# Two PSUM banks that exchange roles each group, eight output products in every slot, and first layers computed transposed

## Chip, cores, metric

The program runs on one core of a Trainium2 chip. The time is that of the device in microseconds. A ratio is the mean time of one kernel's fast runs over that of the kernel before in the same rounds, so it is not quite the ratio of the medians quoted. The kernel before had medians from 864.08 to 867.49 us in these rounds, so runs of different rounds are compared by their ratios.

## The reference, cut to what matters

```python
def mab(q, kv):                                   # softmax(q kv^T / sqrt(128)) kv
    ...
h = mab(inducing, x)                              # 4 batches, 32 rows of 128
x = mab(x, h)                                     # 4 x 12416 rows of 128
g, val = x @ w_gate, x @ w_val                    # 128 -> 1536 twice
ffn = (gelu(g) * val) @ w_out                     # 1536 -> 128
out = x + sigmoid(x @ w_res) * ffn
```

A row of the second attention's result is a mixture of 32 rows of `h`. So the kernel multiplies `h` by `w_gate`, `w_val` and `w_res` once a batch (the "first layers") and mixes the products with each token's 32 weights.

## The kernel before

Tokens go in groups of 512; a batch has 25 groups, its last a short one. A group has 12 chunks of 128 hidden columns, taken two at a time: six slots. A slot has a gate pair G (PE, then gelu `ge` on ACT), a value pair V (PE, then `u = ge*V` on DVE), and a share of the 48 output products `ffn += u.T @ wO`. Once a group PE also mixes rows for the sigmoid (`hr`, read by ACT as `th`) and for the residual (`ha`, read by ACT as `at`), and DVE forms `th = (th+1)*ffn`.

```python
ps_gv = ... bufs=3   # three tiles of two banks, shared by G, V and most else
ps_f  = ... bufs=1   # one bank: ffn
ps_m  = ... bufs=1   # one bank: mixes, accumulation of h, small work
...
for gi in range(ngrp):                            # f is the group's first slot
    ...
        at(f + 4, lg.gate)                        # mix for th, then th on ACT
        at(f + 6, lg.residual)                    # mix for at
        for i, n in enumerate((10, 10, 10, 9, 9)):
            at(f + 3 + i, lambda lg=lg, n=n: lg.mms(n))
        at(f + 7, lg.end)                         # th on DVE, add on POOL, store
...
bg(13 + i, 2, ...accumulate...)                   # bg(g, p): group g of the batch, slot p
bg(18, 2, finish_h); bg(19, 2, turn_h)
bg(20, 2, first_layer(hg, columns 0:1024)); bg(22, 2, first_layer(hv, 0:1024))
bg(23, 2, first_layer(hg and hv, 1024:1536)); bg(22, 5, res_layer)
...
            pe.matmul(bank[:, o:o + e - c], ht_t[b], w[:, c:e], start=True, stop=True)
                act.activation(dst[:, c0:c1], bank[:, o0:o], AC.Copy, bias=0.0, scale=0.5)
```

Products of a group stand in its slots 3, 4, 5 and in slots 0 and 1 of the next; slot 2 has none, and there the work for the next batch's `h` is put. Two bursts a batch compute all scores; after each, the number of gates that run ahead of values starts at one and grows by one every second group, up to four, so some groups have a seventh gate.

The softmax here doesn't subtract the row's maximum and nothing guards it: scores larger than these inputs give would overflow.

Of the kernel before, what the change touches and what calls it, by code (L numbers as in the profile page):

```python
# [18 lines left out]
def kernel(  # L19
# [49 lines left out]
    p_sm = ctx.enter_context(tc.tile_pool(name="soft", bufs=2))  # L69
    p_h = ctx.enter_context(tc.tile_pool(name="hpool", bufs=2))  # L70
    p_ge = ctx.enter_context(tc.tile_pool(name="gelu", bufs=6))
    p_u = ctx.enter_context(tc.tile_pool(name="up", bufs=8))
    p_fin = ctx.enter_context(tc.tile_pool(name="fin", bufs=2))
    ps_gv = ctx.enter_context(tc.tile_pool(name="psgv", bufs=3, space=bass.MemoryType.PSUM))
    ps_f = ctx.enter_context(tc.tile_pool(name="psf", bufs=1, space=bass.MemoryType.PSUM))
    ps_m = ctx.enter_context(tc.tile_pool(name="psm", bufs=1, space=bass.MemoryType.PSUM))

    ctx.enter_context(tc.manual_schedule())

    def misc_bank():  # L80
        return ps_m.tile([P, TOK], FP32, name="ms", tag="ms")

    def wide_bank():
        return ps_gv.tile([P, 2 * TOK], FP32, name="gv", tag="gv")
# [71 lines left out]
    def accumulate(b, j0, j1, first, last):  # L156
        if first:
            acc_t[b] = misc_bank()
        acc = acc_t[b]
        for j in range(j0, j1):  # L160
            k, jj = divmod(j, PRE)
            cq = j % Q
            o = acc[cq * M:(cq + 1) * M, :]
            e = e_of.pop(("a", b, j))
            pe.matmul(o[:, 0:P], e, hi_t[b, k][:, jj, :],
                      start=(first and j < j0 + Q), stop=False, skip_group_check=True)
            pe.matmul(o[:, P:2 * P + 1], e, lo_t[b, k][:, jj, :P + 1],
                      start=False, stop=(last and j + Q >= j1), skip_group_check=True)
        if last:
            if b not in nacc_t:  # L170
                nacc_t[b] = p_h.tile([P, 2 * P + 1], FP32, name="nacc", tag="nacc", bufs=1)
                ve.tensor_copy(nacc_t[b], acc[:, :2 * P + 1])
            else:
                na = nacc_t[b]
                ve.tensor_tensor(na, acc[:, :2 * P + 1], na, AL.add)
            del acc_t[b]

    def finish_h(b):
        hs = misc_bank()
        na = nacc_t.pop(b)  # L180
        sm = strips.rearrange("p q m -> p (q m)")
        pe.matmul(hs[:, P:P + 1], sm, na[:, 2 * P:2 * P + 1], start=True, stop=True)
        pe.matmul(hs[:, 0:P], sm, na[:, 0:P], start=True, stop=False)
        pe.matmul(hs[:, 0:P], sm, na[:, P:2 * P], start=False, stop=True)
        rz = p_h.tile([P, 1], FP32, name="rz1", tag="rz1")
        ve.reciprocal(rz, hs[:, P:P + 1])
        hf = p_h.tile([P, P], FP32, name="hf", tag="hf", bufs=1)
        ve.tensor_scalar(hf, hs[:, 0:P], rz, None, op0=AL.mult)
        hf_t[b] = hf
        ha = p_h.tile([P, P], FP16, name="ha", tag="ha")  # L190
        ha_t[b] = ha
        po.tensor_copy(ha, hf)
        po.tensor_tensor(ha[M:2 * M, :], hf[M:2 * M, :], ha[M:2 * M, :], AL.subtract)
        hg_t[b] = p_h.tile([P, F], BF16, name="hg", tag="hg")
        hv_t[b] = p_h.tile([P, F], BF16, name="hv", tag="hv")

    def turn_h(b):
        tp = misc_bank()
        pe.transpose(tp[:, :P], hf_t.pop(b), ident)
        ht = p_h.tile([P, P], FP16, name="ht", tag="ht")  # L200
        ve.tensor_copy(ht, tp[:, :P])
        ht_t[b] = ht

    def first_layer(b, parts, engs):
# [3 lines left out]
        for (dst, w, c0, c1), eng in zip(parts, engs):  # L208
# [7 lines left out]
            else:  # L216
                ve.tensor_scalar(dst[:, c0:c1], bank[:, o0:o], 0.5, None, op0=AL.mult)

    def res_layer(b):
        bank = misc_bank()  # L220
        pe.matmul(bank[:, :P], ht_t[b], wR, start=True, stop=True)
        hr = p_h.tile([P, P], FP16, name="hr", tag="hr")
        hr_t[b] = hr
        act.activation(hr, bank[:, :P], AC.Copy, bias=0.0, scale=1.0)
        ve.tensor_tensor(hr[M:2 * M, :], bank[M:2 * M, :P], hr[M:2 * M, :], AL.subtract)  # L225
# [82 lines left out]
    class Last:  # L308
# [9 lines left out]
        def mms(self, n):  # L318
            per = self.slots[0][1]
            for _ in range(min(n, len(self.todo))):  # L320
                fc, k = self.todo.pop(0)
                first = self.ffn is None
                if first:
                    self.ffn = ps_f.tile([P, TOK // P, P], FP32, name="ffn", tag="ffn")
                si, c = divmod(fc, per)
                o = c * self.tw + k * P

                pe.matmul(self.ffn[:, k, :], u_t[self.gi, si][:, o:o + P], wO[:, fc, :],  # L328
                          start=first, stop=not self.todo, skip_group_check=True)
                if k == self.nk - 1 and (c == per - 1 or fc == FCH - 1):  # L330
                    del u_t[self.gi, si]

        def mix(self, h):
            bank = misc_bank()
            r = slice(0, 2 * M)
            for k in range(self.nk):
                pe.matmul(bank[:, k * P:(k + 1) * P],  # L337
                          rt_t[self.b, self.k][r, self.j0 + k, :],
                          h[r, :], start=True, stop=True)
            return bank  # L340
# [108 lines left out]
    for j0 in range(PRE, nblk, 4 * PRE):  # L449
        j1 = min(j0 + 4 * PRE, nblk)  # L450
        norm_b(0, j0, j1, exp_b(0, j0, j1))
    warm = ps_f.tile([P, TOK // P, P], FP32, name="ffn", tag="ffn")
    for i in range(10):
        pe.matmul(warm.rearrange("p k c -> p (k c)"), wG[:, :P], wG[:, :TOK],
                  start=True, stop=True)



# [9 lines left out]
    bursts = {}  # L468
    LEAD = 4

    def at(i, f):
        windows.setdefault(i, []).append(f)

    for gi in range(ngrp):
        lg = Last(gi)
        f = first[gi]
        if len(groups[gi][4]) == 6:
            at(f + 4, lg.gate)
            at(f + 6, lg.residual)
            for i, n in enumerate((10, 10, 10, 9, 9)):  # L480
                at(f + 3 + i, lambda lg=lg, n=n: lg.mms(n))
            at(f + 7, lg.end)
        else:
            at(f + 1, lg.gate)
            at(f + 3, lg.residual)
            at(f + 3, lambda lg=lg: lg.mms(len(lg.todo)))
            at(f + 3, lg.end)

    def plan(b):
        nb = b + 1  # L490
        i0 = first[b * gpb]

        def bg(g, p, f):
            at(i0 + 6 * g + p, f)

        if b == 0:
            for i in range(1, ntile):
                bg(0, 1 + (9 * i) // 2, lambda i=i: weights_b(0, i))
        if nb < B:
            for k in range(ntile):  # L500
                i = (9 * k) // 2 + 1
                bg(1, i, lambda k=k: fetch(nb, k))
                bg(1, i + 5, lambda k=k: convert(nb, k, po, po))
                bg(1, i + 8, lambda k=k: turn(nb, k))

            bursts[i0 + 6 * 12 + 2] = [
                (lambda j0=j0: exp_a(nb, j0, min(j0 + 4 * PRE, nblk)))
                for j0 in range(0, nblk, 4 * PRE)]
            cuts = [0, 20, 40, 60, 80, nblk]
            for i, (j0, j1) in enumerate(zip(cuts, cuts[1:])):  # L510
                bg(13 + i, 2, lambda j0=j0, j1=j1: accumulate(nb, j0, j1, True, True))
            bg(18, 2, lambda: finish_h(nb))
            bg(19, 2, lambda: turn_h(nb))
            e2s = []

            def piece(j0, j1):
                e2s.append((j0, j1, exp_b(nb, j0, j1)))
            bursts[i0 + 6 * 21 + 2] = [
                (lambda j0=j0: piece(j0, min(j0 + 4 * PRE, nblk)))
                for j0 in range(0, nblk, 4 * PRE)]  # L520
            for i in range(4):
                bg(21, 3 + i, lambda: norm_b(nb, *e2s.pop(0)))
            bg(20, 2, lambda: first_layer(nb, [(hg_t[nb], wG, 0, cw)], [act]))
            bg(22, 2, lambda: first_layer(nb, [(hv_t[nb], wV, 0, cw)], [act]))
            bg(23, 2, lambda: first_layer(
                nb, [(hg_t[nb], wG, cw, F), (hv_t[nb], wV, cw, F)], [act, act]))
            bg(22, 5, lambda: res_layer(nb))
            for i in range(ntile):
                j = 6 * 21 + 5 + (5 * i) // 2
                at(i0 + j, lambda i=i: weights_b(nb, i))  # L530

    for b in range(B):
        plan(b)
# [10 lines left out]
        sent["v"] += 1  # L544

    def window_next():
        for f in windows.pop(sent["w"], []):
            f()
        sent["w"] += 1

# [22 lines left out]
            gate_next()  # L573
            lead, since = 1, 0
    assert not bursts
    for i in sorted(windows):
        for f in windows[i]:
            f()


# [28 lines left out]
```

## Time and profile before

The median was 867.49 us in the rounds with the changed kernel (864.56 to 869.95).

| | busy | share of 863.7 us |
|---|---|---|
| DVE | 798.7 us | 92% |
| PE (ends are modelled) | 789.5 us | 91% |
| ACT | 734.9 us | 85% |
| POOL | 347.6 us | 40% |

Read it as three engines handing three PSUM tiles round. A useful measure, used throughout, is the distance between the starts of DVE's th records of successive groups. It is 7.74 us in a quiet group, 8.62 in one with a seventh gate. A "dip" below is a stretch in which the trace shows the TensorE clock granted at half. The page's lines stand in the prediction.

### The profile page before, as it was taken

The page shows a single profiled execution, that of the slowest core. Times are in us where ns is not written, and L with a number is a line of the kernel's source. Part 1 is how long each engine was busy: PE and PEld are TensorE (multiplying, and loading weights), DVE is VectorE, ACT ScalarE, POOL GpSimd, SP SyncE. Part 2 cuts the span into 40 slices and gives each one's busy share as a digit, 9 for nine tenths or more (in the row PEclk, how much of TensorE's full clock was granted, in tenths as well). Part 3 has the DMA queues.
Part 4 walks back from the last instruction along what each step waited for, and adds up shares of the span by engine and source line. Part 5 has one row for each costly group of instructions (what it writes and reads, how often), then busy time and mean ns, then how long its engine had stood idle before and what let it go on. Part 6 is the DMA issues. An engine that isn't in the chain of part 4 may idle for free.

```text
span 863.7 us, 23212 instructions
## 1 busy us (share of the span) xinstructions
PE 789.5 (91%) x9548; PEld 473.8 (55%) x9548; DVE 798.7 (92%) x784; ACT 734.9 (85%) x870; POOL 347.6 (40%) x304
## 2 busy tenths in 40 slices
PE   5889999999889999999988999999988899999997
PEld 4545556555545555656554555565554555555554
DVE  8689999999989999899988999989998999999997
ACT  5588988989878888898978888989888898889885
POOL 2429885112266776112145787411225711111111
PEclk9599999999999999999989999999999999999999
DMA  8337875010147776101034677410114411100111
GB/s 308 108 70 155 199 171 142 27 38 26 38 98 139 185 184 138 41 26 38 26 69 95 165 181 171 104 39 26 38 34 92 101 39 39 38 32 32 38 38 40
DMA packets 114185, 77.04 MB, mean 89 GB/s; under 512 B 92416, under 2 KB 95136, under 8 KB 114080
## 3 DMA queue, kind: packets, MB, share of 16 engines
q1 hardware_dynamic: 111792, 73.14, 33.5%
q10 hardware_dynamic: 2288, 2.43, 1.0%
q8 instruction: 74, 1.21, 0.6%
q14 instruction: 31, 0.25, 0.1%
HBM read 27.87 MB, written 25.43 MB: 62 GB/s over the span
## 4 chain that ended last, share of the span: by engine, by line
PE 68%; DVE 14%; ACT 11%; issue 5%; DMA 1%; POOL 1%; DVEq 0%; POOLq 0%; SPq 0%; ACTq 0%
PE ffn L328 31%; PE gv L289 30%; ACT ge L298 10%; DVE u L305 9%; PE ms L337 4%; DVE lo L116 1%; DVE hi L114 1%; DVE z L242 1%; DVE th L356 1%; ACT hg L215 1%; DMA ge<-in_moe_w_out_dram 1%; POOL wO L417 0%; PE gv L212 0%; DMA rt<-a 0%; DMA xf<-in_x_dram 0%
## 5 line engine op out<-in xcount | busy, mean ns | idle before, releaser
L305 DVE TENSOR_TENSOR u<-ge,gv 128x1024 bf16<-128x1024 f32 x584 | 693.0, 1214 | 48.4 <-PE gv L289 24.2
L298 ACT ACTIVATE ge<-gv 128x1024 f32<-128x1024 f32 x584 | 586.0, 1021 | 88.4 <-PE gv L289 63.6
L328 PE MATMUL ffn<-wO,u 128*128 128x128 bf16 x4656 | 346.8, 221 | 0.6 <-DVE th L356 0.6
L328 PEld LDWEIGHTS <-u 128*128 128x128 bf16 x4656 | 263.7, 98 | 113.9 <-issue 93.0
L359 POOL TENSOR_TENSOR at<-at,th 128x512 f32<-128x512 f32 (+1 forms) x100 | 124.0, 1240 | 428.3 <-ACT ge L298 361.3
L289 PE MATMUL gv<-rt,hv 64*128 64x512 f16 x1152 | 224.1, 380 | 35.6 <-ACT ge L298 22.7
L289 PE MATMUL gv<-rt,hg 64*128 64x512 f16 x1152 | 225.3, 387 | 8.5 <-ACT ge L298 3.1
L289 PEld LDWEIGHTS <-hv 64*128 64x128 bf16 x1200 | 97.0, 94 | 110.5 <-issue 106.3
L289 PEld LDWEIGHTS <-hg 64*128 64x128 bf16 x1200 | 63.1, 93 | 92.1 <-issue 40.9
L256 POOL TENSOR_TENSOR a<-e,z 128x1024 f16<-128x1024 f32 (+2 forms) x50 | 91.2, 1833 | 27.2 <-DMA rt<-a 14.2
L116 POOL TENSOR_TENSOR lo<-xf,hi 128x1024 f16<-128x1024 f32 x36 | 76.8, 2135 | 0.3
L337 PEld LDWEIGHTS <-rt 64*128 64x128 f16 x768 | 57.6, 94 | 30.8 <-issue 3.6
L356 DVE SCALAR_TENSOR_TENSOR th<-th,ffn 128x512 f32<-128x512 f32 (+1 forms) x100 | 66.5, 665 | 1.0 <-PE ffn L328 1.0
L345 ACT ACTIVATE th<-ms 128x512 f32<-128x512 f32 (+1 forms) x100 | 58.0, 580 | 2.4 <-PE ms L337 2.4
L351 ACT ACTIVATE at<-ms 128x512 f32<-128x512 f32 (+1 forms) x100 | 58.0, 580 | 1.9 <-PE ms L337 1.8
L114 POOL CAST hi<-xf 128x1024 f16<-128x1024 f32 x36 | 37.3, 1037 | 29.5 <-DMA xf<-in_x_dram 19.5
L337 PE MATMUL ms<-ha,rt 64*128 64x128 f16 x384 | 36.6, 215 | 1.1 <-DVE hr L225 1.1
L337 PE MATMUL ms<-hr,rt 64*128 64x128 f16 x384 | 37.5, 219 | 0.0
L141 PEld LDWEIGHTS <-xt 128*128 128x128 f16 x768 | 24.3, 99 | 7.0 <-issue 6.4
L132 ACT ACTIVATE xt<-gv 128x1024 f16<-128x1024 f16 x12 | 12.3, 1024 | 13.3 <-PE gv L131 13.3
L131 PE MATMUL gv<-identF,hi 128*128 128x128 f16 x96 | 11.0, 285 | 9.0 <-DVE hi L114 8.8
L235 ACT ACTIVATE e<-gv 128x1024 f32<-128x1024 f32 (+2 forms) x13 | 11.9, 959 | 7.9 <-PE gv L141 7.8
(88 smaller groups left out, 261.3 us busy)
## 6 DMA issues: line engine op xcount, KB each, us to landing
out_dram<-at SPq DMA_DIRECT2D x96, 256.0 KB, 2.0
xf<-in_x_dram SPq DMA_DIRECT2D x42, 512.0 KB, 4.3
ge<-in_x_dram SPq DMA_DIRECT2D x6, 512.0 KB, 6.1
rt<-a SPq DMA_TRANSPOSE x49, 3.1
xt<-hi SPq DMA_TRANSPOSE x36, 3.2
ge<-in_moe_w_gate_dram ACTq DMA_DIRECT2D x1, 512.0 KB, 4.5
ge<-in_moe_w_val_dram ACTq DMA_DIRECT2D x1, 512.0 KB, 5.6
ge<-in_moe_w_out_dram ACTq DMA_DIRECT2D x1, 512.0 KB, 4.5
```

The lines of the kernel that those rows point to most:

```text
L114: e_hi.tensor_copy(hi[:, :w, :], xf[:, :w, :])
L116: e_lo.tensor_tensor(lo[:, :w, :P], xf[:, :w, :], hi[:, :w, :], AL.subtract)
L256: po.tensor_tensor(a2[:, :n], ev[:, o:o + n, :].unsqueeze(2).to_broadcast([P, n, Q, M]), z[:, 1, o:o + n].unsqueeze(2).unsqueeze(3).to_bro ...
L289: pe.matmul(v[:, c * tw:(c + 1) * tw], weights[b][r, (c0 + c) * P:(c0 + c + 1) * P], rt[r, :], start=True, stop=True)
L298: act.activation(ge[:, :n], v, AC.Gelu, bias=0.0, scale=1.0)
L305: ve.tensor_tensor(u[:, :n], ge_t.pop((gi, si)), v, AL.mult)
L328: pe.matmul(self.ffn[:, k, :], u_t[self.gi, si][:, o:o + P], wO[:, fc, :], start=first, stop=not self.todo, skip_group_check=True)
L337: pe.matmul(bank[:, k * P:(k + 1) * P], rt_t[self.b, self.k][r, self.j0 + k, :], h[r, :], start=True, stop=True)
L345: act.activation(self.th[:, :self.tw], bank[:, :self.tw], AC.Tanh, bias=0.0, scale=0.5)
L351: act.activation(self.at[:, :self.tw], bank[:, :self.tw], AC.Copy, bias=0.0, scale=1.0)
L356: ve.scalar_tensor_tensor(self.th[:, :tw], self.th[:, :tw], 1.0, self.ffn.rearrange("p k c -> p (k c)")[:, :tw], AL.add, AL.mult)
L359: po.tensor_tensor(self.at[:, :tw], self.at[:, :tw], self.th[:, :tw], AL.add)
```

## The change

The intent: two banks change roles from group to group, so that a group's products can begin in slot 2, while DVE has yet to read the former group's, and every slot has eight. Work that stood in slot 2 goes to slot 3; the mix for `th` goes behind its slot's products. `res_layer` (the product of `h` and `w_res`) moves from slot 5 of a batch's group 22 to slot 3 of its group 23, and in the short groups the mixes stand later. The first layers of batches 1 to 3 are computed transposed, 32 columns wide (768 in all), by one tile, one ACT copy, POOL copies and DMA transposes.

```diff
-    ps_f = ... name="psf", bufs=1
-    ps_m = ... name="psm", bufs=1
+    ps_2 = [... name=f"ps{i}", bufs=1 ... for i in range(2)]
+    def side_bank(group):
+        return ps_2[group % 2].tile([P, TOK], FP32, name="sb", tag="sb")
     def misc_bank():
-        return ps_m.tile(...)
+        return side_bank(parity[0] + 1)
...
+        for o, w in ((0, wG), (TOK, wV)):
+            for c in range(FCH):
+                pe.matmul(bank[:, o + c * M:o + (c + 1) * M], w[:, c * P:(c + 1) * P],
+                          ht_t[b][:, 0:M], start=True, stop=True)
+        act.activation(hgt_t[b], ...768 columns..., AC.Copy, bias=0.0, scale=0.5)
+    def spread(b, i):      # po.tensor_copy to four strips, sy.dma_start_transpose
...
-            at(f + 4, lg.gate)
-            at(f + 6, lg.residual)
-            for i, n in enumerate((10, 10, 10, 9, 9)):
-                at(f + 3 + i, lambda lg=lg, n=n: lg.mms(n))
-            at(f + 7, lg.end)
+            for i in range(6):
+                at(f + 2 + i, lambda lg=lg: lg.mms(8))
+            at(f + 4, lg.gate, END)
+            at(f + 6, lg.residual, START)
+            at(f + 7, lg.end, LATE)
...
-                bg(13 + i, 2, ...accumulate...)
+                bg(13 + i, 3, ...accumulate..., START)     # finish_h, turn_h likewise
-            bg(20, 2, first_layer...); bg(22, 2, ...); bg(23, 2, ...)
+            bg(20, 3, lambda: first_layer_t(nb), START)
+            for i in range(3):
+                bg(20, 5 + i, lambda i=i: spread(nb, i))
-            bg(22, 5, lambda: res_layer(nb))
+            bg(23, 3, lambda: res_layer(nb), START)
```

Within a slot, START stands ahead of the products, END behind them, LATE last. The changed kernel also has seven instead of eight `u` buffers.

More of the change, by code (lines that the diff above doesn't have):

```diff
@@ L71 @@
     p_ge = ctx.enter_context(tc.tile_pool(name="gelu", bufs=6))
-    p_u = ctx.enter_context(tc.tile_pool(name="up", bufs=8))
+    p_u = ctx.enter_context(tc.tile_pool(name="up", bufs=7))
     p_fin = ctx.enter_context(tc.tile_pool(name="fin", bufs=2))
     ps_gv = ctx.enter_context(tc.tile_pool(name="psgv", bufs=3, space=bass.MemoryType.PSUM))
-    ps_f = ctx.enter_context(tc.tile_pool(name="psf", bufs=1, space=bass.MemoryType.PSUM))
-    ps_m = ctx.enter_context(tc.tile_pool(name="psm", bufs=1, space=bass.MemoryType.PSUM))
+    ps_2 = [ctx.enter_context(tc.tile_pool(name=f"ps{i}", bufs=1, space=bass.MemoryType.PSUM))
+            for i in range(2)]
     ctx.enter_context(tc.manual_schedule())
+    parity = [0]
+    def side_bank(group):
+        return ps_2[group % 2].tile([P, TOK], FP32, name="sb", tag="sb")
     def misc_bank():
-        return ps_m.tile([P, TOK], FP32, name="ms", tag="ms")
+        return side_bank(parity[0] + 1)
     def wide_bank():
@@ L217, in first_layer, with first_layer_t @@
                 ve.tensor_scalar(dst[:, c0:c1], bank[:, o0:o], 0.5, None, op0=AL.mult)
+    hgt_t = {}
+    def first_layer_t(b):
+        bank = wide_bank()
+        for o, w in ((0, wG), (TOK, wV)):
+            for c in range(FCH):
+                pe.matmul(bank[:, o + c * M:o + (c + 1) * M], w[:, c * P:(c + 1) * P],
+                          ht_t[b][:, 0:M], start=True, stop=True)
+        hgt_t[b] = p_h.tile([P, 2, FCH * M], BF16, name="hgt", tag="hgt", bufs=1)
+        act.activation(hgt_t[b], bank.rearrange("p (s n) -> p s n", s=2)[:, :, :FCH * M],
+                       AC.Copy, bias=0.0, scale=0.5)
+    def spread(b, i):
+        n = 2 * FCH // 3
+        src = hgt_t[b].rearrange("p s (c m) -> p (s c) m", m=M)[:, i * n:(i + 1) * n, :]
+        a2 = p_sm.tile([P, PRE, Q, M], BF16, name="a2", tag="a2")
+        po.tensor_copy(a2, src.unsqueeze(2).to_broadcast([P, n, Q, M]))
+        for dst, c0, c1 in ((hg_t[b], 0, FCH), (hv_t[b], FCH, 2 * FCH)):
+            lo, hi = max(c0, i * n), min(c1, (i + 1) * n)
+            if lo < hi:
+                sy.dma_start_transpose(
+                    dst.rearrange("p (c f) -> p c f", f=P)[:, lo - c0:hi - c0, :],
+                    a2[:, lo - i * n:hi - i * n].rearrange("p c q m -> p (c q m)"))
     def res_layer(b):
@@ L323, in mms @@
                 if first:
-                    self.ffn = ps_f.tile([P, TOK // P, P], FP32, name="ffn", tag="ffn")
+                    self.ffn = side_bank(self.gi).rearrange("p (k c) -> p k c", c=P)
                 si, c = divmod(fc, per)
@@ L333, in mix @@
         def mix(self, h):
-            bank = misc_bank()
+            bank = side_bank(self.gi + 1)
             r = slice(0, 2 * M)
@@ L451 @@
         norm_b(0, j0, j1, exp_b(0, j0, j1))
-    warm = ps_f.tile([P, TOK // P, P], FP32, name="ffn", tag="ffn")
+    warm = side_bank(0)
     for i in range(10):
-        pe.matmul(warm.rearrange("p k c -> p (k c)"), wG[:, :P], wG[:, :TOK],
-                  start=True, stop=True)
+        pe.matmul(warm, wG[:, :P], wG[:, :TOK], start=True, stop=True)
     flat = [(gi, si) for gi in range(ngrp) for si in range(len(groups[gi][4]))]
@@ L469, with at @@
     LEAD = 4
-    def at(i, f):
-        windows.setdefault(i, []).append(f)
+    START, MIDDLE, END, LATE = range(4)
+    def at(i, f, where=MIDDLE):
+        windows.setdefault(i, []).append((where, f))
     for gi in range(ngrp):
@@ L477 @@
         if len(groups[gi][4]) == 6:
-            at(f + 4, lg.gate)
-            at(f + 6, lg.residual)
-            for i, n in enumerate((10, 10, 10, 9, 9)):
-                at(f + 3 + i, lambda lg=lg, n=n: lg.mms(n))
-            at(f + 7, lg.end)
-        else:
-            at(f + 1, lg.gate)
-            at(f + 3, lg.residual)
+            for i in range(6):
[3 more added lines that the diff above has]
+            at(f + 7, lg.end, LATE)
+        else:
+            at(f + 2, lg.gate, END)
             at(f + 3, lambda lg=lg: lg.mms(len(lg.todo)))
-            at(f + 3, lg.end)
+            at(f + 3, lg.residual, END)
+            at(f + 3, lg.end, LATE)
     def plan(b):
@@ L491, in plan, with bg @@
         i0 = first[b * gpb]
-        def bg(g, p, f):
-            at(i0 + 6 * g + p, f)
+        def bg(g, p, f, where=END):
+            at(i0 + 6 * g + p, f, where)
         if b == 0:
@@ L510, in plan @@
             for i, (j0, j1) in enumerate(zip(cuts, cuts[1:])):
-                bg(13 + i, 2, lambda j0=j0, j1=j1: accumulate(nb, j0, j1, True, True))
-            bg(18, 2, lambda: finish_h(nb))
-            bg(19, 2, lambda: turn_h(nb))
+                bg(13 + i, 3, lambda j0=j0, j1=j1: accumulate(nb, j0, j1, True, True), START)
+            bg(18, 3, lambda: finish_h(nb), START)
+            bg(19, 3, lambda: turn_h(nb), START)
+            bg(20, 3, lambda: first_layer_t(nb), START)
+            for i in range(3):
+                bg(20, 5 + i, lambda i=i: spread(nb, i))
             e2s = []
@@ L522, in plan @@
                 bg(21, 3 + i, lambda: norm_b(nb, *e2s.pop(0)))
-            bg(20, 2, lambda: first_layer(nb, [(hg_t[nb], wG, 0, cw)], [act]))
-            bg(22, 2, lambda: first_layer(nb, [(hv_t[nb], wV, 0, cw)], [act]))
-            bg(23, 2, lambda: first_layer(
-                nb, [(hg_t[nb], wG, cw, F), (hv_t[nb], wV, cw, F)], [act, act]))
-            bg(22, 5, lambda: res_layer(nb))
+            bg(23, 3, lambda: res_layer(nb), START)
             for i in range(ntile):
                 j = 6 * 21 + 5 + (5 * i) // 2
-                at(i0 + j, lambda i=i: weights_b(nb, i))
+                at(i0 + j, lambda i=i: weights_b(nb, i), END)
     for b in range(B):
@@ L546, in window_next @@
     def window_next():
-        for f in windows.pop(sent["w"], []):
+        i = sent["w"]
+        if i < nflat:
+            parity[0] = flat[i][0]
+        for _, f in sorted(windows.pop(i, []), key=lambda e: e[0]):
             f()
@@ L575 @@
     assert not bursts
-    for i in sorted(windows):
-        for f in windows[i]:
-            f()
+    while windows:
+        window_next()
 _INS = ['x', 'inducing', 'moe_w_gate', 'moe_w_val', 'moe_w_out', 'moe_w_res']
```

## The prediction

> **What bounds the kernel now.** I read the page's busy table, then the quiet stretches, then one group of six slots instruction by instruction, then the places where groups are long.
>
> ```profile
> PE 789.5 (91%) x9548; PEld 473.8 (55%) x9548; DVE 798.7 (92%) x784; ACT 734.9 (85%) x870; POOL 347.6 (40%) x304
> ...
> L305 DVE TENSOR_TENSOR u<-ge,gv 128x1024 bf16<-128x1024 f32 x584 | 693.0, 1214 | 48.4 <-PE gv L289 24.2
> ```
> ```profile
> 740.00:780.00 40.00, 38.19 (x419) 22.44 (x418) 39.08 (x37) 35.46 (x43) 6.38 (x5) 1.00 0.09 35
> ```
>
> The second fence is a quiet stretch of the last batch (columns: stretch, length, PE, PEld, DVE, ACT, POOL busy, clock, DMA share, GB/s). DVE seems full there, 39.08 of 40 us. It isn't. Two u products back to back last 2.35 us in the timeline, so an undisturbed step from u to u is 2.35 - 1.22 = 1.13 us. Six steps and the th instruction (0.60 us to the next u) are 7.38 us; the distance between L356 records of successive groups is 7.74 us. Some 0.35 us a group is waiting in gaps too short to be listed. One group, its times counted from 107.36, the start of its first u:
>
> ```profile
> 107.36 7.23 DVE L305 TENSOR_TENSOR u<-ge,gv 128x1024 bf16<-128x1024 f32 x6
> ...
> 108.55 0.39 PE L289 MATMUL gv<-rt,hg 64*128 64x512 f16 x2
> ...
> 108.78 0.38 PE L289 MATMUL gv<-rt,hv 64*128 64x512 f16 x2
> ...
> 108.99 0.38 PE L337 MATMUL ms<-hr,rt 64*128 64x128 f16 x4
> 109.03 1.02 ACT L298 ACTIVATE ge<-gv 128x1024 f32<-128x1024 f32 x1 [0.61 <-PE gv L289]
> ...
> 109.31 0.73 PE L328 MATMUL ffn<-wO,u 128*128 128x128 bf16 x10
> ...
> 109.95 0.59 ACT L345 ACTIVATE th<-ms 128x512 f32<-128x512 f32 x1
> 109.97 0.39 PE L289 MATMUL gv<-rt,hg 64*128 64x512 f16 x2
> ...
> 110.43 2.20 ACT L298 ACTIVATE ge<-gv 128x1024 f32<-128x1024 f32 x2
> ...
> 111.51 0.39 PE L289 MATMUL gv<-rt,hv 64*128 64x512 f16 x2
> ...
> 111.73 0.38 PE L337 MATMUL ms<-ha,rt 64*128 64x128 f16 x4
> ...
> 112.04 0.68 PE L328 MATMUL ffn<-wO,u 128*128 128x128 bf16 x9
> ...
> 112.65 0.39 PE L289 MATMUL gv<-rt,hg 64*128 64x512 f16 x2
> ...
> 112.88 0.38 PE L289 MATMUL gv<-rt,hv 64*128 64x512 f16 x2
> ...
> 114.50 0.68 DVE L356 SCALAR_TENSOR_TENSOR th<-th,ffn 128x512 f32<-128x512 f32 x1
> ```
>
> Call a gate pair G, a value pair V. Three wide PSUM tiles are shared by G and V in turn, so G waits until DVE has left the tile of two values before (u start to G: 108.55 - 107.36 = 1.19), and V waits until ACT has left the tile of the gate before the last one (ge start to V: 111.51 - 110.43 = 1.08). With G to ge 0.48 and V to u 0.50 one turn of this ring is 1.19 + 0.48 + 1.08 + 0.50 = 3.25 us, against three DVE steps of 3.39: hardly any slack. The chain through th sets the first stall: u 0, G 1.19, ge 1.67, th 2.59 (ACT was busy until then), the next ge 3.07, V 4.15, u 4.65 instead of 4.52. The second is PE's: behind that V stand the L337 mix (0.31 with its change of tile shape), 9 products and G, so the next V comes at 112.88, 1.37 later, its u at 6.02, th at 7.15 (114.50 - 107.36 = 7.14). The 7.74 is thus reproduced to 0.02 us.
>
> **What the skill says.** "Vector Engine (DVE) Microarchitecture Reference", section 5.2, gives 1.0417 ns per column and about 75 ns an instruction: 1.14 us for 1024 columns; the trace's 1.13 agrees, so DVE's floor can't move. "TensorE: Matmul & The Clock Gate", "Wait - 56ns, not 53.3ns?", gives 55.6 ns between warm 128-column matmuls; here ten products hold the next G by 0.66 us and nine by 0.61, so about 0.055 each and 0.11 for changing shape: agrees. "Perfetto Trace Analysis", "Optimization Strategy", reads consistent bubbles as a possible lack of buffers: here the ring of three tiles, which the change leaves alone.
>
> **The change, part by part.**
>
> *Order on the engines.* Compared instruction by instruction, ACT and DVE keep their steady order; only PE's changes. Products go 8 to each slot instead of 10, 10, 10, 9, 9 and none. The th mix (L337 with hr) moves behind the products of its slot; the residual mix stays ahead of them. The second bank only allows products in the once empty slot before DVE's th has read the former group's; before, PE waited 0.6 us for that in the whole run.
>
> *Steady group.* An 8-product slot holds the next G by 0.31 + 0.44 + 0.11 = 0.86 after V. Start again at u 0. The once empty slot now delays its following G, its ge, and the V after G, which comes at about 1.50 instead of 1.42. Then: change of shape and 8 products, mix at 1.50 + 0.86 = 2.36. The lag from one L221 matmul to ACT's L224 was 242.11 - 241.81 = 0.30; with three more matmuls 0.46, so th starts at 2.82 instead of 2.59, and becomes PE-bound. The next ge is then at 2.82 + 0.48 = 3.30, V 4.38, u 4.88 instead of 4.65. Behind that V one product less saves 0.06, so the last u comes at 4.88 + 1.31 = 6.19, and the group is 6.19 + 1.13 + 0.60 = 7.92, rounded errors apart 7.90. That is +0.16 us. Some 50 groups are of this kind (22 in the last batch, 8 to 10 in each other): +8 us.
>
> *Groups with an extra gate* (8.62 us, lead growing by one). Their V behind two gates waits for a ge anyway, which hides the new products; I work out +0.05 for a dozen: +0.6 us.
>
> *Accumulation, finish_h, turn_h* move from slot 2 to slot 3. There they stood where no products were: 40 matmuls from 155.92 to the next G at 156.61, 0.69 us, and the groups cost 7.84 to 7.86, just 0.1 more than a quiet one. Now that slot holds them and 8 products: the next G comes 0.5 later, so the mix, th, ge and u after it, less what the extra DVE instruction (0.42) hides anyway: +0.3 to +0.5 us for each of 5 + 2 windows in three batches: +6 to +10 us, I take 8.
>
> *First layers of batches 1 to 3.* Removed per batch: six 512-column matmuls, ACT's four copies (L215: 6.5 + 4.9 us in all, means 0.81, so 4 x 0.81 = 3.25 us) and two of three wide tiles. Added: 24 matmuls of 32 columns (32 such took 0.95 us, so 0.7), one ACT copy of 768 columns (between 0.59 for 512 and 1.02 for 1024: about 0.8), three POOL copies of about 1.04 (the L114 row; POOL is 40% busy), four transposes of about 3.1 us on a queue that has room. Nothing of the last two is needed until the next batch's first group, four groups later. What is gained on the path: the group with the value layer took 8.88 without the clock dip, and should be about 7.9 (-1.0); the one with the two half layers 9.28, should be 8.7 (-0.6); the one with the first gate layer keeps a wide tile and an ACT copy (0). -1.6 x 3 = -5 us.
>
> Sum: 869.3 + 8 + 0.6 + 8 - 5 = 881 us.
>
> **The rivals.** (1) The even spread pays, as the change intends: the slot after the residual mix loses a product, PE gets ahead, and the 0.35 us of stall shrinks. For it: the second stall (0.23) is PE's, and PE is not at its limit. If both stalls went, 97 x 0.35 = 34 us, 835 us; half of it, with the first layers, 847. Against it: the heaviest slot keeps its mix and loses only one product, and the ring of three tiles stays, so PE can't get ahead. (2) The th mix isn't late, because V or ACT runs differently from my fixed point: then the steady group stays at 7.74 or loses 0.06, and only first layers and accumulations count: 862 to 870. (3) The half clock after the second burst of a batch (two of three batches in this trace; 11.19 and 11.31 us against 8.88, so 2.3 us each) goes or spreads: minus 5, or plus 2 for the third batch.
>
> **Range and chances.** My sum says 881. It rests on a lag of 0.46 us and a shape change of 0.11 us assumed for an order not yet seen, and such a change is rarely made without a reason, so I pull it to 877. 8 in 10: 857 to 889. Slower by over 2% is above 886.6: 0.2. Faster by over 2% is below 851.9, which needs rival 1: 0.11. Within: 0.69.
>
> **What will show it.** In the quiet stretch of the last batch, the distance of DVE's th records: 7.90 if I am right, 7.4 to 7.7 for rival 1, 7.74 for rival 2. ACT's th should begin about 2.8 us after the first u and wait for PE, not ACT. Groups with accumulation should take 8.2 to 8.4 instead of 7.86. The two groups after the second burst should be 1.0 and 0.6 shorter, and ACT's first-layer copies one of about 0.8 us a batch. The prediction is wrong if PE's order lets V come earlier behind the mix, or if the batches' clock dips change by more than one.

## The result and the profile after

The changed kernel took 876.53 us (875.85 to 876.92) against 867.49; the ratio is 1.0105 (95%: 1.0066 to 1.0143). That is about 1% slower and within the 2% band; the forecast was 877.

First the page and a quiet stretch of the changed kernel. The second fence has the columns of the prediction's stretch.

```profile
PE 790.8 (90%) x9602; PEld 470.8 (54%) x9602; DVE 798.3 (91%) x784; ACT 737.0 (84%) x861; POOL 357.6 (41%) x313
...
L338 DVE TENSOR_TENSOR u<-ge,gv 128x1024 bf16<-128x1024 f32 x584 | 692.4, 1215 | 59.8 <-PE gv L322 45.6
...
L378 ACT ACTIVATE th<-sb 128x512 f32<-128x512 f32 (+1 forms) x100 | 58.4, 584 | 19.2 <-PE sb L370 11.1
```
```profile
740.00:780.00 40.00, 37.20 (x402) 21.66 (x400) 38.08 (x36) 35.31 (x41) 6.36 (x5) 1.00 0.09 35
```

DVE does the same 798 us of work in a longer span, and waits 45.6 us for V pairs in gaps that are long enough to be listed, where it was 24.2. ACT's th, which waited 2.4 us in the whole run before, now waits 19.2. The line of th before:

```profile
L345 ACT ACTIVATE th<-ms 128x512 f32<-128x512 f32 (+1 forms) x100 | 58.0, 580 | 2.4 <-PE ms L337 2.4
```

A quiet group of the changed kernel, from the timeline; count from 751.91, its first u:

```profile
751.91 4.61 DVE L338 TENSOR_TENSOR u<-ge,gv 128x1024 bf16<-128x1024 f32 x4
...
753.39 0.39 PE L322 MATMUL gv<-rt,hv 64*128 64x512 f16 x2
753.66 1.02 ACT L331 ACTIVATE ge<-gv 128x1024 f32<-128x1024 f32 x1 [0.36 <-PE gv L322]
...
753.72 0.62 PE L361 MATMUL sb<-wO,u 128*128 128x128 bf16 x8
...
754.27 0.28 PE L370 MATMUL sb<-hr,rt 64*128 64x128 f16 x2
...
754.76 0.60 ACT L378 ACTIVATE th<-sb 128x512 f32<-128x512 f32 x1
...
755.26 1.94 ACT L331 ACTIVATE ge<-gv 128x1024 f32<-128x1024 f32 x2
...
756.33 0.39 PE L322 MATMUL gv<-rt,hv 64*128 64x512 f16 x2 [0.33 <-ACT ge L331]
...
756.83 2.52 DVE L338 TENSOR_TENSOR u<-ge,gv 128x1024 bf16<-128x1024 f32 x2 [0.30 <-PE gv L322]
...
759.26 0.68 DVE L389 SCALAR_TENSOR_TENSOR th<-th,sb 128x512 f32<-128x512 f32 x1
```

V is at 1.48, the mix only at 2.36, behind eight products; th is at 2.85, when ACT has been free since 2.67 (753.66 + 0.92, the step between two ge records, - 751.91); the next ge is at 3.35, V at 4.42, u at 4.92. DVE has a gap of 0.30 us there; in the group before no gap was long enough to be listed (its u stood at 4.65).

Where the 11.4 us between the two profiled spans (875.1 - 863.7) went, by sums of the distances between th records:

| groups | before | changed | difference |
|---|---|---|---|
| 49 quiet | 380.1 | 389.7 | +9.6 |
| 9 with a seventh gate only | 77.6 | 77.5 | -0.1 |
| 21 with accumulate, finish_h, turn_h | 173.0 | 185.3 | +12.3 |
| 6 with bursts | 68.1 | 69.4 | +1.3 |
| 3 + 3 + 3 with first layers before (20, 22, 23) | 85.9 | 75.8 | -10.1 |
| short groups and last | 17.6 | 17.6 | 0.0 |
| up to the first th | 57.7 | 56.1 | -1.6 |

The row of the first layers also holds dips. Before, group 22 took 11.19 and 11.31 us in the two batches with a dip and 8.88 in the one without; after, 8.73 and 8.73 with and 7.73 without. That is 4.7 us of dips before and 2.0 after, so 2.7 of the 10.1 us come from shorter dips. The stretches, first of the kernel before, then of the changed one (the number behind POOL's is the clock):

```profile
233.80:240.60 6.80, 5.74 (x34) 2.95 (x33) 5.06 (x5) 3.89 (x5) 4.97 (x3) 0.50 0.23 64
442.00:448.80 6.80, 6.08 (x36) 3.08 (x37) 4.72 (x5) 3.55 (x5) 4.97 (x3) 0.50 0.29 74
...
241.40:244.80 3.40, 3.40 (x24) 1.94 (x24) 2.53 (x3) 1.84 (x3) 3.40 (x3) 0.50 0.23 83
661.20:664.60 3.40, 3.40 (x27) 2.10 (x28) 2.81 (x3) 1.77 (x3) 3.40 (x2) 0.51 0.36 107
```

### The profile page after: what moved, and what is told of

Same layout as the page of the kernel before. It is cut to its first block, busy times and chain, and to the rows that moved or that the text cites. A ratio compares the mean times of both kernels' runs of the same rounds, so it can differ in the third digit from the quotient of the medians.

```text
span 875.1 us, 23358 instructions
## 1 busy us (share of the span) xinstructions
PE 790.8 (90%) x9602; PEld 470.8 (54%) x9602; DVE 798.3 (91%) x784; ACT 737.0 (84%) x861; POOL 357.6 (41%) x313
## 4 chain that ended last, share of the span: by engine, by line
DVE 39%; PE 29%; ACT 17%; issue 13%; DMA 1%; DVEq 1%; POOL 0%; ACTq 0%; POOLq 0%; SPq 0%
DVE u L338 30%; ACT ge L331 16%; PE gv L322 15%; PE sb L361 9%; DVE th L389 5%; PE sb L370 2%; DVE lo L123 2%; DVE z L275 1%; DVE hi L121 1%; PE sb L172 1%; PE sb L174 1%; DVEq L338 1%; PE gv L148 0%; DMA xf<-in_x_dram 0%; DMA rt<-a 0%
## 5 line engine op out<-in xcount | busy, mean ns | idle before, releaser
L338 DVE TENSOR_TENSOR u<-ge,gv 128x1024 bf16<-128x1024 f32 x584 | 692.4, 1215 | 59.8 <-PE gv L322 45.6
L361 PE MATMUL sb<-wO,u 128*128 128x128 bf16 x4656 | 361.9, 221 | 0.2 <-DVE u L338 0.2
L322 PE MATMUL gv<-rt,hg 64*128 64x512 f16 x1152 | 238.3, 386 | 10.1 <-DVE u L338 8.3
L322 PEld LDWEIGHTS <-hg 64*128 64x128 bf16 x1200 | 70.4, 93 | 65.9 <-issue 16.9
L378 ACT ACTIVATE th<-sb 128x512 f32<-128x512 f32 (+1 forms) x100 | 58.4, 584 | 19.2 <-PE sb L370 11.1
L389 DVE SCALAR_TENSOR_TENSOR th<-th,sb 128x512 f32<-128x512 f32 (+1 forms) x100 | 66.5, 665 | 1.1 <-PE sb L361 1.1
L384 ACT ACTIVATE at<-sb 128x512 f32<-128x512 f32 (+1 forms) x100 | 60.2, 602 | 2.2 <-PE sb L370 2.2
L370 PEld LDWEIGHTS <-rt 64*128 64x128 f16 x768 | 50.2, 94 | 21.8 <-issue 1.1
L370 PE MATMUL sb<-hr,rt 64*128 64x128 f16 x384 | 38.2, 220 | 0.5 <-DVE ht L208 0.5
L370 PE MATMUL sb<-ha,rt 64*128 64x128 f16 x384 | 36.6, 215 | 0.0
L139 ACT ACTIVATE xt<-gv 128x1024 f16<-128x1024 f16 x12 | 12.3, 1023 | 13.5 <-PE gv L138 13.5
L138 PE MATMUL gv<-identF,hi 128*128 128x128 f16 x96 | 10.5, 276 | 10.1 <-DVE hi L121 10.0
```

Of the source, the lines that this page charges most:

```text
L322: pe.matmul(v[:, c * tw:(c + 1) * tw], weights[b][r, (c0 + c) * P:(c0 + c + 1) * P], rt[r, :], start=True, stop=True)
L338: ve.tensor_tensor(u[:, :n], ge_t.pop((gi, si)), v, AL.mult)
L361: pe.matmul(self.ffn[:, k, :], u_t[self.gi, si][:, o:o + P], wO[:, fc, :], start=first, stop=not self.todo, skip_group_check=True)
L370: pe.matmul(bank[:, k * P:(k + 1) * P], rt_t[self.b, self.k][r, self.j0 + k, :], h[r, :], start=True, stop=True)
L378: act.activation(self.th[:, :self.tw], bank[:, :self.tw], AC.Tanh, bias=0.0, scale=0.5)
L384: act.activation(self.at[:, :self.tw], bank[:, :self.tw], AC.Copy, bias=0.0, scale=1.0)
```

## The experiments

All ten runs gave right results. The medians, and distances between th records in each profile:

| run | median us | ratio | quiet group | 21 accumulation groups, mean |
|---|---|---|---|---|
| before | | 1 | 7.74 | 8.24 |
| changed | 876.53 | 1.0105 | 7.95 | 8.83 |
| narrow layers only | 854.29 | 0.9879 | 7.74 | 8.24 |
| changed, wide layers | 880.50 | 1.0178 | 7.95 | 8.83 |
| changed, mix for th first | 864.59 | 1.0007 | 7.76 | 8.83 |
| changed, old counts | 892.39 | 1.0321 | 8.04 | 9.11 |
| before, accumulations one slot later | 880.44 | 1.0186 | 7.74 | 9.12 |
| before, narrow layers, 12/8/12/2/14 | 871.35 | 1.0093 | 7.98 | 8.39 |
| changed, fixed banks | 926.57 | 1.0718 | 8.65 | 9.14 |
| changed, mix first, 8/8/8/8/2/14 | 858.98 | 0.9933 | 7.59 | 8.80 |
| the same, accumulations in slot 2 | 853.48 | 0.9849 | 7.59 | 8.55 |
| the same, res_layer group as changed | 853.06 | 0.9850 | 7.59 | 8.55 |

### 1. The narrow first layers alone

```diff
 (kernel before)
+    first_layer_t and spread of the changed kernel; u buffers 8 -> 7
-            bg(20, 2, first_layer...); bg(22, 2, ...); bg(23, 2, ...)
+            bg(20, 2, lambda: first_layer_t(nb))
+            for i in range(3): bg(20, 5 + i, lambda i=i: spread(nb, i))
```

> The kernel before with only the narrow first layers of batches 1 to 3 added (products, banks and mixes as before). My theory: this part alone is a gain. In the changed kernel the groups with the value layer and the two half layers are 1.15 us (without clock dips) and 1.5 us shorter, so 3 x 2.65 = 8 us less than before, about 860 us, ratio 0.991; quiet groups stay at 7.74 us and accumulation groups at 8.35/8.62/7.86. Rival: those groups are shorter because products fill the slot that was empty there; then this kernel gains at most 2 us (ratio 0.998 to 1.0).

854.29 us against 865.00, ratio 0.9879 (0.9859 to 0.9900). Quiet and accumulation groups are those of before to 0.01 us. Group 22 without a dip took 8.35 instead of 8.88, group 23 8.04 instead of 9.28: 3 x 1.8 = 5.3 us. The rest of the 10.1 us between the profiled th records is mostly half clock: one dip of 0.66 us in group 22 where there were two of 2.3 and 2.4. So this part alone is a gain. What the layers themselves give is less than the 8 us I expected (5.3 us, since group 22 fell by 0.53 and not 1.15); the total is more, by the clock. The seven u buffers are in this run too and leave quiet groups at 7.74. How often dips come varies from run to run: the granted clock was 0.984 to 0.987 in the runs of this kernel and 0.973 to 0.983 in those of the kernel before; that the narrow layers shorten the dips was seen in these profiles, not tested by itself.

### 2. The changed kernel with the wide layers

```diff
 (changed kernel)
-            bg(20, 3, lambda: first_layer_t(nb), START)   # and spread
+            bg(20, 3, first_layer(hg, 0:1024), START); bg(22, 3, first_layer(hv, 0:1024), START)
+            bg(23, 3, first_layer(hg and hv, 1024:1536), START)
```

> The changed kernel with the wide first layers put back (one slot later, as its accumulations are). My theory: banks, spread and moved windows alone cost the sum of quiet groups (+9.6), accumulation groups (+12.4) and bursts (+1.3): about 23 us less 1.5 at the start, so about 888 us, ratio 1.024 against before; 8 to 11 us slower than the changed kernel. Rival (the narrow layers do nothing by themselves): 877 us.

880.50 us, ratio 1.0178, so 0.7% slower than the changed kernel's 1.0105, where I expected 0.9 to 1.3%. Quiet and accumulation groups stay at 7.95 and 8.83: all that the change does besides the layers makes that loss. My 888 was too high mainly by group 22, which I had left as before: it takes 8.05 us on average here, 7.2 us less in three batches. The dips that are missing account for 4.7 us of that; the rest came although the wide value layer is still there, and `res_layer` is not.

### 3. The mix for th ahead of its slot's products

```diff
-            at(f + 4, lg.gate, END)
+            at(f + 4, lg.gate, START)
```

> The changed kernel with the mix for th ahead of the eight products of its slot, nothing else. My theory (th is late because its mix stands behind products): th starts when ACT is free, about 2.66 us after the first u instead of 2.85, and quiet groups fall from 7.95 to 7.76 us or so: 49 x 0.19 = 9 us less. Accumulation groups may gain up to 0.3 us each or nothing, as the mix then waits for DVE to have read the bank: about 863 to 868 us, ratio 0.994 to 1.0. Rival (eight products in the once empty slot are what delays the group): quiet groups stay at 7.95, 876 us.

864.59 us, ratio 1.0007 (0.9981 to 1.0032). One word in the schedule takes back the whole net loss. In the timeline of its quiet group, counted from 757.50:

```profile
759.19 0.38 PE L370 MATMUL sb<-hr,rt 64*128 64x128 f16 x4
759.24 1.02 ACT L331 ACTIVATE ge<-gv 128x1024 f32<-128x1024 f32 x1 [0.36 <-PE gv L322]
...
760.16 0.59 ACT L378 ACTIVATE th<-sb 128x512 f32<-128x512 f32 x1
```

The mix is at 1.69 and th at 2.66, the moment ACT is free, and the group takes 7.76 us as worked out. The products in slot 2 are still there, so they don't cause the 7.95. Groups with a seventh gate even fall from 8.61 to 8.38. Accumulation groups stay at 8.83 on average, because those with a seventh gate fall (9.30 to 9.08) and those without rise (8.38 to 8.64). In nine of the 21 PE's mix now waits for DVE to have read the bank, 4.8 us in all.

### 4. The old counts in the changed kernel

```diff
-            for i in range(6): at(f + 2 + i, ...mms(8))
+            for i, n in enumerate((10, 10, 10, 9, 9)): at(f + 3 + i, ...mms(n))
```

> The changed kernel with the old counts of products (10, 10, 10, 9, 9 and none), the mix for th still behind the products. My theory: th then comes behind 10 products instead of 8 and is no earlier (first V 0.08 earlier, products 0.11 later), and the residual mix has a product more behind it: quiet groups 8.0 to 8.05 us, about 4 us slower than the changed kernel, 880 us. Rival (the spread costs): quiet groups return to 7.74 us, 866 us.

892.39 us: the quiet group is 8.04 us as worked out, so the spread isn't the culprit; with the mix behind ten products it is worse. The total was missed by 12 us: accumulation groups rose to 9.11 (slot 3 holds ten products and the accumulation), groups with a seventh gate to 8.94, neither of which I had counted.

### 5. The kernel before with its accumulations one slot later

```diff
 (kernel before)
-    bg(13 + i, 2, ...accumulate...); bg(18, 2, finish_h); bg(19, 2, turn_h)
+    bg(13 + i, 3, ...accumulate...); bg(18, 3, finish_h); bg(19, 3, turn_h)
```

> The kernel before with only the accumulations, finish_h and turn_h moved from the slot without products to the next one, which has ten. My theory: the move by itself delays the mix, th, ge and u behind it; the accumulation groups without a further gate go from 7.86 to about 8.4 us, the 21 groups together cost 8 to 11 us, quiet groups stay at 7.74: about 874 us, ratio 1.01. Rival (it is the bank that changes roles, or the products in the once empty slot, that make accumulation groups long in the changed kernel): no change, 865 us.

880.44 us, ratio 1.0186. The 21 groups cost 18.6 us more, all others nothing but for a dip: the move by itself costs, without banks or spread. It was larger than I said. The accumulation stands behind ten products here and ahead of eight in the changed kernel, so this doesn't say how much of the changed kernel's loss is the move's. Two waits, from the timeline of one such group, show why:

```profile
177.22 1.02 ACT L298 ACTIVATE ge<-gv 128x1024 f32<-128x1024 f32 x1 [1.24 <-PE gv L289]
...
177.65 0.38 PE L337 MATMUL ms<-hr,rt 64*128 64x128 f16 x4 [0.25 <-DVE nacc L175]
```

ACT stands idle 1.24 us until PE has done ten products and 40 accumulation matmuls, and then PE waits for DVE to have read the bank that the mix needs.

### 6. Few products behind the late V, in the kernel before

```diff
 (kernel of experiment 1)
-            for i, n in enumerate((10, 10, 10, 9, 9)):
+            for i, n in enumerate((12, 8, 12, 2, 14)):
```

> The kernel before with the narrow first layers and with its products laid 12, 8, 12, 2, 14 instead of 10, 10, 10, 9, 9: few behind the residual mix, whose V comes late. My theory (the second stall is PE's, and only the slot with the late V matters, not evenness): the V after it comes 0.9 instead of 1.37 us later, the u behind it needn't wait, quiet groups 7.57 us, 49 x 0.17 = 8 us less than the narrow layers alone: about 846 us, ratio 0.978. Rival (DVE and ACT set the 7.74, PE doesn't): 854 us, ratio 0.988.

871.35 us: my theory failed here. The quiet group is 7.98, not 7.57. Its timeline, counted from 760.70:

```profile
761.18 0.39 PE L315 MATMUL gv<-rt,hv 64*128 64x512 f16 x2 [0.55 <-ACT ge L324]
...
761.50 0.84 PE L354 MATMUL ffn<-wO,u 128*128 128x128 bf16 x12
762.28 0.39 PE L315 MATMUL gv<-rt,hg 64*128 64x512 f16 x2
...
763.68 0.59 ACT L371 ACTIVATE th<-ms 128x512 f32<-128x512 f32 x1
```

What was taken from one slot fell on its neighbours. Behind 14 products the gate of slot 2 and its ge come late, V waits for that ge, and behind 12 products the next G comes at 1.58 instead of 1.19. th is then at 2.98 instead of 2.59. The slot in front of the th chain matters as much as the one behind the late V, and with slot 2 empty the other four slots must take 46 products. Other counts were not tried.

### 7. Banks that don't change roles

```diff
 (changed kernel)
-    side_bank(self.gi) for ffn; side_bank(group + 1) for all else
+    side_bank(0) for ffn; side_bank(1) for all else
```

> The changed kernel with one bank always for products and the other always for all else, products still 8 to each slot. My theory: the first products of a group must then wait for DVE's th of the former group, 0.75 us on PE in every group, and the gates behind them come later: quiet groups about 8.6 us, some 34 us more, 905 to 915 us. Rival (the exchange of banks isn't needed): 876 us.

926.57 us with quiet groups of 8.65 us. In the list of waits (total us, times, longest) of this kernel stands:

```profile
PE sb L361 <- DVE th L389: 59.3, 96, 2.5
```

The page of the changed kernel has 0.2 us of idle time before its products. So the exchange of banks does what it is meant to do: without it products in slot 2 wait for DVE's th. The total is above my range because groups with accumulations (+6.7 us), first layers (+4.7) and bursts (+4.5) rose as well.

### 8. The exchange of banks, used for an uneven spread

```diff
 (changed kernel)
-            for i in range(6): at(f + 2 + i, ...mms(8))
+            for i, n in enumerate((8, 8, 8, 8, 2, 14)): at(f + 2 + i, ...mms(n))
-            at(f + 4, lg.gate, END)
+            at(f + 4, lg.gate, START)
```

> The changed kernel with the mix for th first in its slot and products 8, 8, 8, 8, 2, 14. My theory: as in the one before, the u behind the residual mix needn't wait: quiet groups 7.6 us instead of 7.76 with eight each, 8 us less: about 857 us. Rival: 865 us.

858.98 us, ratio 0.9933; the quiet group is 7.59. With eight products in slot 2 the slots ahead of th are light enough, and the failed idea of experiment 6 works: behind the residual mix PE reaches the next V 0.98 us after the last, where it was 1.31 in experiment 3. From the timeline of this kernel:

```profile
759.10 0.39 PE L322 MATMUL gv<-rt,hv 64*128 64x512 f16 x2
...
760.08 0.39 PE L322 MATMUL gv<-rt,hv 64*128 64x512 f16 x2
```

### 9 and 10. Accumulations back in slot 2

```diff
 (kernel of experiment 8)
-            bg(13 + i, 3, accumulate, START)           # finish_h, turn_h, in 9 res_layer too
+            bg(13 + i, 2, accumulate in the group's own product bank, START)
+            in these groups products 0, 0, 12, 14, 6, 16
 (10 alone)
+            group 23: products and res_layer as in 8, lg.gate at END
```

> As the run with products 8, 8, 8, 8, 2, 14 and the mix first, but in the eight groups a batch that carry an accumulation, finish_h, turn_h or res_layer, those go back to slot 2 in the group's own product bank, and its products wait until slot 4 (none, none, 12, 14, 6, 16). My theory (an accumulation costs what it and products in one slot push onto the mix, th and ge behind it, or what the mix waits for the bank): these groups fall from 8.47 to about 7.9 to 8.0 and from 9.2 to about 8.6, the res_layer group from 8.85 to 8.3; 24 groups by 0.5 us, 12 us less: about 847 us, ratio 0.979. Rival (DVE's own extra work of 0.42 us sets those groups): at most 3 us less, 856 us.

853.48 us, ratio 0.9849 (0.9810 to 0.9889). The accumulation groups fell to 8.29 and 8.90, from 8.47 and 9.21 (group 18 by 0.43, group 13 not at all), not by the half microsecond I expected, and what holds them isn't settled. The group of res_layer grew to 10.23 us, against the expectation.

> As the former run, but the res_layer group goes back to eight-eight-eight-eight-two-fourteen products, with its mix for th behind them, as in the changed kernel, where it took 7.77 us instead of the 10.23 of the former run. My theory: 3 x 2.3 = 7 us less at best (8.0 us for that group), about 847 us, ratio 0.978, ahead of the kernel before and of the narrow layers alone (0.988). Rival (the res_layer group needs its eight products and the bank of before to be short): about 3 us less, ratio 0.982.

853.06 us, ratio 0.9850 (0.9818 to 0.9883). The res_layer group is back at 8.15 to 8.27, near the 8.0 worked out, but the median didn't move, and 847 was missed: this profile has more half clock (granted 0.979; the other runs had 0.978 to 0.987, those of experiment 9 0.982 to 0.987), and a burst group of 10.91 us.

Something else holds these kernels back that I had overlooked. Group 11 of the first batch took 10.28 us in experiment 8 and 9.78 in 9, not 7.59. In 9 the clock is full there; from its timeline:

```profile
140.73 0.60 ACT L385 ACTIVATE th<-sb 128x512 f32<-128x512 f32 x1 [2.08 <-POOL at L399]
```

ACT can't write th until POOL has read an older one (there are two buffers), and POOL, which also converts the next batch's tokens there, is late. The same wait of 2.1 us is in experiment 8; experiment 3, with slower groups, has none.

The kernels of experiments 9 and 10 are ahead of the kernel before by 1.5%, and not to be told from the narrow layers alone (0.9879) by these intervals.

## Why the prediction was right

The time was right to 0.5 us, and that closeness is luck. My own sum was 881, on a base of 869.3 (the median of three runs; 867.49 with the fourth), and I had pulled it to 877 out of caution. Its terms came to +11.6 us, and the profiled spans differ by 11.4, but only because errors cancel: quiet groups, accumulations and bursts cost 23.2 us, where I had 16, and first layers and the start gave back 11.7, where I had 5. Step by step:

**The ring and the chain through th: right.** (The 1.14 us that I gave from the skill for 1024 columns is an estimate; the trace's 1.13 decides.) The worked group had V at 1.50, th at 2.82, the next ge at 3.30, u at 4.88 and 7.90 us in all; measured were 1.48, 2.85, 3.35, 4.92 and 7.95. Experiment 3 shows the cause by taking it away, and experiment 4 by making it worse, each with a quiet group within 0.05 us of what the same arithmetic gave beforehand. The quiet groups cost 9.6 us instead of 8, as the step was 0.21 and not 0.16 us. The lag of 0.46 from the mix to ACT was 0.49; the first ge came at 1.75 instead of 1.67, as G stands behind the products of slot 2, which I had left out.

**Groups with a seventh gate: right,** -0.1 us for +0.6.

**Accumulations: right in kind, too small.** I said +0.3 to +0.5 for each and took 8 us in all; it was 0.59 on average and 12.3 us. The mis-sized term is that of the nine groups that have a seventh gate besides: I gave them the same, and they rose by 0.68 to 0.75 (8.62 to 9.30 and 9.37). The other twelve rose by 0.43 to 0.53 (7.86 to 8.38, within the 8.2 to 8.4 foretold). In one of the nine, from the timeline of the changed kernel, ACT stands idle until PE has done 40 accumulation matmuls and eight products:

```profile
168.37 1.02 ACT L331 ACTIVATE ge<-gv 128x1024 f32<-128x1024 f32 x1 [1.13 <-PE gv L322]
```

Why a seventh gate adds to it isn't shown. Nor is it shown how much of the 0.59 is the late mix, which these groups share with the quiet ones (+0.21). Experiment 5 shows that such a move costs; experiments 9 and 10, which undo it with other counts, win back 0.25 us of it on average.

**First layers: right in sign, mis-sized.** I gave -1.0, -0.6 and 0 for groups 22, 23 and 20; it was -1.15 (without dips), -1.51 and +0.21. The -1.0 was near for only half of a reason: the change also takes `res_layer` out of group 22, which I left out. With the narrow layers alone (experiment 1) that group fell by 0.53; with `res_layer` moved and the wide value layer kept (experiment 2) it fell by 0.83. No run moves `res_layer` by itself. The failed step is "8.7" for group 23. It has a seventh gate, as I took it to, but the stretch up to its th also holds the short group's last u, which is half as wide. An estimate from 8.62 and the lengths of a wide and a half u (1.22 and 0.69) is 8.1; experiment 1 has 8.04, the changed kernel 7.77. The half u, from the changed kernel's list by shapes:

```profile
L338 DVE TENSOR_TENSOR u<-ge,gv 128x512 bf16<-128x512 f32 x4 | 2.8, 688 | 0.0
```

ACT's copy and POOL's copies cost what was said, by the groups of the changed kernel:

```profile
L244 POOL COPY a<-hgt 128x1024 bf16<-128x1024 bf16 x9 | 9.2, 1039 | 12.6 <-DMA hg<-a 8.2 <-ACT hgt L236 4.3
L236 ACT ACTIVATE hgt<-gv 128x768 bf16<-128x768 f32 x3 | 2.4, 810 | 2.0 <-PE gv L233 2.0
```

**Left out:** bursts (+1.3 us), and the start (-1.6), which varies with the half-clock stretches: experiment 1, with the order of before, has 56.35 us there, experiment 5 58.12, the kernel before 57.73.

**The rivals.** Rival 1, that evenness pays: refuted for quiet groups (experiment 3: 7.76 with eight each against 7.74), though it is worth 0.24 us in groups with a seventh gate. But my argument against it, that PE can't get ahead of the ring, was too strong: experiment 8 gets 0.15 us by an uneven spread that uses the exchanged banks. Rival 2, th not late: refuted by the timeline. Rival 3, the half clock: two batches have a dip in both profiles, but it costs 2.7 us less in group 22.

So the expected gain of the even spread never was on the path of a quiet group; what was on it is the place of one mix of four matmuls. Moved behind the products, it cost about as much as the narrow layers gained (9.6 us in the quiet groups, 10.1 in the groups of the layers, dips included).

## What to carry to other kernels

When engines hand a few buffers round in a ring, write down one turn with measured lags, and find which instruction waits last; evening out the load of an engine that has time to spare gained nothing in the quiet groups here, but moving a short instruction, which another engine waits for, behind a long row of others costs what that engine then stands idle (here it made a group 0.21 us longer). Before moving background work to another slot, look at what stood in its old place: an empty slot may have been what hid it. Test the parts of a mixed change apart: here one was a gain of 1.2% and the other a loss of 1.8%. They don't add up to the 1.05% of both together: each of the two profiles has fewer dips than the kernel before, and that gain counts only once. And an engine that looks idle can still hand back a buffer late: in experiments 8 and 9 POOL, busy for some 40% of the span, did so once, for 2.1 us.

## What the Trainium skill lacked or had wrong

- "TensorE: Matmul & The Clock Gate", "Back-to-back issue gap", puts matmuls of 128 columns about 81 ns apart in a real kernel's stream of weight loads and matmuls. Here each product has a weight load of its own, and twelve of them take 0.84 us with the last one's 0.22: 0.056 us apart, close to the 55.6 ns that the page gives for back-to-back matmuls, as cited in the prediction.
- No page that I found has a figure for going from 128-row products to 64-row pairs and back; "TensorEngine Tiling (Array Packing)", "Key Properties", says only that a change of tiling mode drains the engine. Here it is about 0.11 us, an estimate: ten products hold the next G by 0.66 us.
- "TensorE: Matmul & The Clock Gate", "Single matmul latency", gives (398 + N)/2.4 ns warm, 0.22 us at 128 columns, which is the duration of the record (0.22; its end is modelled). ACT started on such a result 0.30 us after the matmul's start, and 0.49 after the start of the mix of four. Lags of this kind (0.48 and 0.50 of the 3.25 us of a ring's turn) have to be read from a trace.
- "Perfetto Trace Analysis", "Optimization Strategy", says that consistent bubbles can mean too few buffers. They need not: with the same banks and wide tiles the quiet group was 7.59, 7.76, 7.95 or 8.04 us by the order of PE's instructions alone.
